# Decode attention over a cached window: all transpositions and scores of a set ahead of the preceding set's V products

## The chip, the cores and the metric

The kernel runs on one core of a Trainium2 chip. The metric is device time in microseconds (us) of one execution, from its first to its last instruction with what lies around them; the median of three runs is 198.4 us (198.16 to 198.71). Engines: TensorE (PE; its weight loads are counted apart as PEld), VectorE (DVE), ScalarE (ACT), GpSimd (POOL) and SyncE (SP), which here only issues DMAs. 16 DMA engines move data between memory and SBUF.

## The reference, cut to what matters

```python
# A: one new token per batch entry, 32 query heads on 8 key/value heads, the last 4096 of 16384 cache rows
q = (x @ wq)                                       # B=4, D=512, Dh=128
k = k_cache[:, :, Sk - 4096:, :];  v = v_cache[:, :, Sk - 4096:, :]
o = softmax(q @ k.T * Dh**-0.5) @ v                # each of 8 kv heads serves 4 query heads
a = o @ wo
# B: a gated two-layer network of the same token
gate = x @ W_gate; up = x @ W_up                   # F = 1792
b = ((gate * (gate > 0)) * up) @ W_down
g = sigmoid((x * gate_w).sum(-1))
out = g * a + (1 - g) * b
```

Nearly all bytes are the two cache windows: 4 x 8 heads x 4096 rows x 128 values in bf16, once for K and once for V, 67 MB of the 81 MB that are read.

## The kernel before, in words

**Tiling.** The 32 pairs of batch entry and kv head are cut into 8 sets of four heads (`NSET`). For each set one DMA loads 4 MB of K into `Ksb[:, s % 2]` and one loads 4 MB of V into `Vsb[:, s % 2]`: 128 partitions of 32 KB each. So there are two K buffers and two V buffers.

**A pass** is one trip through `for s in range(NSET)` (L524). It works on the K of set `s` and on the V of set `s - 1`:

- `kt(s, i)`, i = 0 to 7 (L393): eight PE transpositions (L400) into one of two PSUM tiles `tr`, then one copy back over K in SBUF, by ACT for i in `ACT_TAKES` = 0, 2, 4, 6, 7 (L406), by DVE for 1, 3, 5 (L408). `kt(s, i)` needs the copy of `kt(s, i - 2)`, because of the two tiles.
- `scores(s, bank)`, bank = 0 to 3 (L410): eight matmuls (L422), after the copies of `kt(s, 2*bank)` and `kt(s, 2*bank + 1)`. After banks 1 and 3 DVE adds the mask and takes the maximum (L428); bank 2 needs the first of these two to have read the tile.
- `maximum(s)` (L432): DVE, one PE product (L436), DVE; `exponent(s, k)`, k = 0, 1 (L445): ACT; `turn(s, k)`, k = 0, 1 (L452): DVE transposes the probabilities into `pT`.
- `values(s, k)`, k = 0 to 3 (L457): sixteen matmuls each (L465) of `pT` with V, into the tile `ob`; after the last ACT copies it out (L471).
- `combine(s)` (L474): small PE products (L479, L483) and DVE scaling; `queries(s)` (L383): POOL prepares the query tile.

**The order of the work** is written out by hand. Each engine runs its list in program order; PE, ACT and DVE run the passes as a hardware loop of two passes per turn. L527 to L550 is that order. The pass of set 0 also runs `maximum`, `values` and so on for set -1 and -2, on nothing of use, so that all turns of the loop are alike.

**The loads** all come from SP, in one list: K0; then for s = 1 to 7 K(s) and V(s-1); then W_gate and W_up (into the K buffer 0), V7, W_down, and five pieces of wo, which wait for nothing. SP waits ahead of each load for the buffer to be free, and a wait holds all loads behind it. L267: K(s) waits for `("SC", s - 2, 3)`, the last score matmul of set s - 2. L271: V(s-1) waits for `("PV", s - 3, 3)`, the last V product of set s - 3.

**What SP really waits for.** Each event counts up a semaphore for one kind of receiver. `SC` and `PV` count for DVE and ACT. For another receiver, `need` (L115) takes the next event of that engine in program order that counts for it:

```python
if by is not None and s[1] not in (kind, "all"):
    s = (by, kind)
    n = 1 + sum(1 for k in self.history[s] if k < at)
```

SP is of kind "x". In the passes PE has two events of that kind, ahead of the change: `TOP(s)`, the first transposition of `kt(s, 0)` (L402), and `CMB(s)`, the first product of `combine(s)` (L480). After the score matmuls of bank 3 in pass s - 2 the next is `TOP(s - 1)`, so K(s) waits for the first transposition of the next pass. That transposition itself waits for the arrival of K(s - 1), and is behind `values(s - 3, 3)` and `maximum(s - 2)` on PE. V(s-1) waits for the same `TOP(s - 1)`. W_gate and W_up wait for `TOP(7)`, W_down for `CMB(6)` behind the last pass.

**After the passes** come `maximum`, `exponent` and `turn` of set 7, `combine(6)`, the first layer of B, `values(7, ...)`, `combine(7)`, and the products with W_down and wo (L576, L565), then two copies (L594, L596) and the store.

Of the kernel before, what the change touches and what calls it, by code (L numbers as in the profile page):

```python
# [181 lines left out]
def bass_gated_mix__sliding_block_cached__glu_gated_reglu__decode_kernel(  # L182
# [13 lines left out]
    with ExitStack() as ctx:  # L196
# [196 lines left out]
        def kt(s, i):  # L393
            bk = TR[i % 2]
            for cc in range(8):
                c = 8 * i + cc
                w = []
                if cc == 0:
                    w = [("K", s), ("KTC", s, i - 2) if i >= 2 else ("KTC", s - 1, i - 2 + NFILL)]
                P.op("pe", lambda e, cc=cc, c=c: e.transpose(  # L400
                    bk[:, cc * 128:(cc + 1) * 128], Kw[:, s % 2, c * 128:(c + 1) * 128], identw[:, :]),
                    ("KT", s, i) if cc == 7 else ("TOP", s) if cc == 0 and i == 0 else None, w,  # L402
                    to="x" if cc == 0 else "act" if i in ACT_TAKES else "dve")
            dst = Kw[:, s % 2, i * 1024:(i + 1) * 1024]
            if i in ACT_TAKES:
                P.op("act", lambda e: e.copy(dst, bk[:, :]), ("KTC", s, i), [("KT", s, i)], to="pe")  # L406
            else:
                P.op("dve", lambda e: e.tensor_copy(dst, bk[:, :]), ("KTC", s, i), [("KT", s, i)], to="pe")  # L408

        def scores(s, bank):  # L410
            bk = SCB[bank % 2]
            pair = bank // 2
            k4 = Ksb[:, s % 2, :].rearrange("p (c k o) -> p c k o", k=128, o=2)
            for o in range(2):
                for a in range(4):
                    w = []
                    if a == 0 and o == 0:
                        w = [("KTC", s, 2 * bank + u) for u in range(2)] + [("QS", s)]
                        w.append(("SCC", s, 0) if pair else ("SCC", s - 1, 1))
                        if bank == 0:  # L420
                            w.append(("NEGMAX", s - 1))
                    P.op("pe", lambda e, a=a, o=o: e.matmul(  # L422
                        bk[32 * a:32 * a + 32, 0:512], qS[:, s % 2, 32 * o:32 * o + 32],
                        k4[:, 16 * bank:16 * bank + 16, 32 * a:32 * a + 32, o], start=(o == 0), stop=(o == 1),
                        tile_position=(0, 32 * a)),
                        ("SC", s, bank) if (a == 3 and o == 1 and bank % 2) else None, w, to="dve")
            if bank % 2:
                P.op("dve", lambda e: e.tensor_tensor_reduce(  # L428
                    sc[:, s % 2, pair * 1024:(pair + 1) * 1024], SCP[:, :], mask[:, :], 1.0, LOWEST, ALU.add, ALU.max,
                    mx[:, s % 2, pair:pair + 1]), ("SCC", s, pair), [("SC", s, bank)], to="dve" if pair else "pe")  # L430

        def maximum(s):  # L432
            par = s % 2
            P.op("dve", lambda e: e.tensor_reduce(mcol[:, par:par + 1], mx[:, par, :], AXIS.X, ALU.max),  # L434
                 ("MCOL", s), [("SCC", s, 1)], to="pe")
            P.op("pe", lambda e: e.matmul(SCB[0][:, 0:128], mcol[:, par:par + 1].to_broadcast([128, 128]), identw[:, :],  # L436
                                          start=True, stop=True),
                 ("MT", s), [("MCOL", s)], to="dve")
            P.op("dve", lambda e: e.tensor_tensor_reduce(  # L439
                mrow[:, :], SCB[0][:, 0:128], qmask[:, :], -SCALE, -LOWEST, ALU.add, ALU.min, negmax[:, par:par + 1]),  # L440
                ("NEGMAX", s), [("MT", s)], to="act")
# [3 lines left out]
        def exponent(s, k):  # L445
            par = s % 2
            P.op("act", lambda e: e.activation(  # L447
                sc[:, par, k * PW:(k + 1) * PW], sc[:, par, k * PW:(k + 1) * PW], ACTF.Exp,
                bias=negmax[:, par:par + 1], scale=SCALE, accum_out=rowsum[:, par, k:k + 1]),
                ("EXP", s, k), [("NEGMAX", s)], to="dve")  # L450

        def turn(s, k):  # L452
            par = s % 2
            P.op("dve", lambda e: e.transpose(pT[:, par, k * PW:(k + 1) * PW], sc[:, par, k * PW:(k + 1) * PW]),  # L454
                 ("PTT", s, k), [("EXP", s, k)], to="pe")

        def values(s, k):  # L457
            par = s % 2
            for c in range(16):
                g = c % 4  # L460
                w = []
                if c == 0:
                    w = [("PTT", s, k * NPIECE // 4), ("V", s), ("OSB", s - 1)]
                blk = 16 * k + c
                P.op("pe", lambda e, c=c, g=g, blk=blk: e.matmul(  # L465
                    OB[32 * g:32 * g + 32, 0:256], pT[:, par, 32 * blk:32 * blk + 32],
                    Vsb[:, par, 256 * blk:256 * blk + 256],
                    start=(k == 0 and c < 4), stop=(k == 3 and c >= 12), tile_position=(0, 32 * g)),
                    ("PV", s, k) if c == 15 and k == 3 else None, w, to="act")
            if k == 3:  # L470
                P.op("act", lambda e: e.copy(osb[:, par, :], OB[:, 0:256]), ("OSB", s),  # L471
                     [("PV", s, 3)], to="pe")

        def combine(s):  # L474
            par, b, half = s % 2, s // 2, s % 2
            r = slice(64 * half, 64 * half + 64)
            for k in range(8):
                lo = 3 - k % 4 + 64 * (k // 4)
                P.op("pe", lambda e, k=k, lo=lo: e.matmul(FB[r, 384:416], Wsel[:, lo:lo + 64], osb[:, par, 32 * k:32 * k + 32],  # L479
                                                          start=(k == 0), stop=(k == 7)), ("CMB", s) if k == 0 else None,  # L480
                     [("OSB", s)], to="x")
            for k in range(NPIECE):
                P.op("pe", lambda e, k=k: e.matmul(FB[r, 416:417], Wsum[:, :], rowsum[:, par, k:k + 1],  # L483
                                                   start=(k == 0), stop=(k == NPIECE - 1)),
                     ("SUMS", s) if k == NPIECE - 1 else None, [], to="dve")
            P.op("dve", lambda e: e.reciprocal(recip[r, par:par + 1], FB[r, 416:417]), ("RECIP", s), [("SUMS", s)], to="dve")  # L486
            if s >= NSET - 2:
                P.op("dve", lambda e: e.tensor_scalar(oq[r, 32 * b:32 * b + 32], FB[r, 384:416], recip[r, par:par + 1],
                                                      gsb[r, b:b + 1], op0=ALU.mult, op1=ALU.mult),
                     ("OQ", s), [("RECIP", s)], to="pe")  # L490
                return
            P.op("dve", lambda e: e.tensor_scalar(otmp[r, :], FB[r, 384:416], recip[r, par:par + 1], None, op0=ALU.mult),  # L492
                 ("OQ", s), [("RECIP", s)], to="x")
            if s >= 0 and half == 1:
                P.op("pool", lambda e: e.tensor_scalar(oq[:, 32 * b:32 * b + 32], otmp[:, :], gsb[:, b:b + 1], None, op0=ALU.mult),  # L495
                     ("OQP", s), [("OQ", s)], to="all")
# [27 lines left out]
        for s in range(NSET):  # L524
            if s % 2 == 0:
                P.turn_edge()
            maximum(s - 1)  # L527
            kt(s, 0)
            kt(s, 1)
            exponent(s - 1, 0)  # L530
            kt(s, 2)
            turn(s - 1, 0)
            exponent(s - 1, 1)
            scores(s, 0)
            combine(s - 2)
            if s + 1 < NSET:
                queries(s + 1)
            kt(s, 3)
            turn(s - 1, 1)
            kt(s, 4)  # L540
            scores(s, 1)
            kt(s, 5)
            kt(s, 6)
            scores(s, 2)
            values(s - 1, 0)
            kt(s, 7)
            values(s - 1, 1)
            values(s - 1, 2)
            scores(s, 3)
            values(s - 1, 3)  # L550
        P.turn_edge()
        maximum(NSET - 1)
        for k in range(NPIECE):
# [105 lines left out]
```

## Time and profile before

| what | value |
|---|---|
| median of 3 runs | 198.4 us |
| the profiled execution: its own time | 197.82 us |
| its span, first to last instruction | 196.6 us |
| PE busy, x instructions | 138.3 us (70%), x1752 |
| DVE busy | 79.8 us (41%) |
| ACT busy | 70.1 us (36%) |
| POOL busy | 14.2 us (7%) |
| bytes read | 81.01 MB, 412 GB/s over the span |
| mean granted PE clock | 0.912 |
| chain that ended last: DMA | 61% |
| chain that ended last: PE, DVE, ACT | 19%, 13%, 4% |

The span is cut into 40 slices of 4.9 us on the page, and other views give any stretch. The chain is followed back from the last instruction: each piece names what was waited for. "issue" is time in which nothing was waited for that the profile shows. In rows of the timeline the first number is the start in us from the start of the span, the second the time taken; `x8` counts instructions, and in brackets stands the idle time of the engine ahead of them with what ended it. SPq rows are SP handing a DMA to its queue, not the transfer.

### The profile page before, as it was taken

What the parts mean: (1) busy time and instruction counts of PE and PEld (TensorE: products, weight loads), DVE (VectorE), ACT (ScalarE), POOL (GpSimd) and SP (SyncE); (2) the same over time, 40 slices, a digit from 0 to 9 for tenths busy, and PEclk for the clock granted to TensorE, in tenths of its full rate; (3) what the DMA queues carried; (4) which work ended last, traced back from release to release, by engine and by line L of the source; (5) the groups of instructions that cost most, each with busy time, mean ns of one, the idle gap of its engine ahead of it and who ended that gap; (6) DMA issues with size and microseconds to landing.
All of it is one profiled execution on the core that took longest, in us unless ns stands there. A gap on an engine that the chain in (4) does not pass through costs nothing.

```text
span 196.6 us, 3919 instructions
## 1 busy us (share of the span) xinstructions
PE 138.3 (70%) x1752; PEld 103.7 (53%) x1752; DVE 79.8 (41%) x127; ACT 70.1 (36%) x97; POOL 14.2 (7%) x34
## 2 busy tenths in 40 slices
PE   0145598879769789973988599759986988603964
PEld 0112476567647557751866387629664765403713
DVE  0000058257435925733176346432663582560001
ACT  1105082355228426440452255224522823500011
POOL 6393000000000000100000001000000000000000
PEclk9999999999999999999699969985999999985555
DMA  6999999969999999999999999999999989998991
GB/s 214 440 440 460 453 440 423 433 270 427 440 443 440 427 433 433 427 427 427 427 427 427 427 427 427 440 440 447 440 433 440 433 381 429 477 427 382 422 401 50
DMA packets 3879, 81.10 MB, mean 413 GB/s; under 512 B 409, under 2 KB 930, under 8 KB 1058
## 3 DMA queue, kind: packets, MB, share of 16 engines
q1 hardware_dynamic: 3864, 81.01, 96.5%
q8 instruction: 5, 0.08, 0.2%
q10 hardware_dynamic: 10, 0.01, 0.0%
HBM read 81.01 MB, written 0.00 MB: 412 GB/s over the span
## 4 chain that ended last, share of the span: by engine, by line
DMA 61%; PE 19%; DVE 13%; ACT 4%; issue 1%; SPq 1%; DVEq 0%
DMA Ksb<-in_A_k_cache_dram 49%; DMA Wbig<-in_A_wo_dram 11%; PE tr L400 10%; DVE Ksb L408 5%; DVE zs L428 5%; PE scp L422 4%; ACT Ksb L406 4%; DVE pT L454 2%; PE fb L479 2%; PE scp L565 1%; PE scp L436 1%; PE ob L465 1%; PE fb L483 0%; DVE zs L434 0%; SPq L289 0%
## 5 line engine op out<-in xcount | busy, mean ns | idle before, releaser
L400 PE MATMUL tr<-identw,Ksb 128*128 128x128 f32 x512 | 70.8, 296 | 7.6 <-DMA Ksb<-in_A_k_cache_dram 6.7
L400 PEld LDWEIGHTS tr<-identw,Ksb 128*128 128x128 f32 x512 | 62.2, 152 | 14.9 <-DMA Ksb<-in_A_k_cache_dram 7.9
L406 ACT COPY Ksb<-tr 128x1024 f32<-128x1024 f32 x40 | 40.5, 1012 | 78.2 <-PE tr L400 78.0
L408 DVE COPY Ksb<-tr 128x1024 f32<-128x1024 f32 x24 | 29.4, 1223 | 29.5 <-PE tr L400 29.5
L428 DVE CUSTOM_DVE_ANT_0 zs<-scp,mask 128x1024 bf16<-128x1024 f32 x16 | 19.3, 1205 | 31.2 <-PE scp L422 31.2
L422 PE MATMUL scp<-Ksb,qS 128*32 128x512 bf16 x256 | 20.0, 387 | 13.0 <-DVE Ksb L408 12.1
L465 PE MATMUL ob<-Vsb,pT 128*32 128x256 bf16 x576 | 21.8, 289 | 7.9 <-DMA Vsb<-in_A_v_cache_dram 7.9
L454 DVE STREAM_TRANSPOSE pT<-zs 128x1024 bf16<-128x1024 bf16 x18 | 22.2, 1238 | 1.8 <-ACT zs L447 1.3
L465 PEld LDWEIGHTS ob<-Vsb,pT 128*32 128x32 bf16 x576 | 15.6, 101 | 13.9 <-issue 9.7
L447 ACT ACTIVATE zs<-zs,negmax 128x1024 bf16<-128x1024 bf16 x18 | 20.7, 1150 | 2.0 <-DVE negmax L439 2.0
L422 PEld LDWEIGHTS scp<-Ksb,qS 128*32 128x32 bf16 x256 | 3.9, 95 | 21.2 <-DVE Ksb L408 18.0
L436 PE MATMUL scp<-identw,zs 128*128 128x128 f32 x18 | 4.9, 359 | 12.2 <-DVE zs L434 10.9
L479 PEld LDWEIGHTS fb<-zs 128*64 128x64 f32 x160 | 10.9, 147 | 4.6 <-issue 3.6
L479 PE MATMUL fb<-zs 128*64 128x32 f32 x160 | 12.0, 231 | 0.5 <-ACT zs L471 0.5
L436 PEld LDWEIGHTS scp<-identw,zs 128*128 128x128 f32 x18 | 3.0, 210 | 14.6 <-DVE zs L434 13.1
L471 ACT COPY zs<-ob 128x256 f32<-128x256 f32 x9 | 3.3, 372 | 20.6 <-PE ob L465 20.6
L486 DVE RECIPROCAL recip<-fb 64x1 f32<-64x1 f32 x10 | 1.6, 162 | 17.7 <-PE fb L483 17.7
L384 POOL TENSOR_TENSOR qS<-zs,cmask 128x64 bf16<-128x64 bf16 x8 | 2.4, 306 | 66.8 <-PE tr L400 64.7
L341 PE MATMUL fb<-identw,zs 5*128 5x5 f32 x4 | 0.6, 262 | 8.9 <-POOL zs L308 8.9
L350 DVE RECIPROCAL gsb<-ez 128x4 f32<-128x4 f32 x1 | 0.2, 178 | 16.0 <-POOL ez L349 16.0
L495 POOL TENSOR_SCALAR oq<-otmp,gsb 128x32 bf16<-128x32 f32 x3 | 1.1, 364 | 71.4 <-DVE otmp L492 71.4
L439 DVE CUSTOM_DVE_ANT_0 mrow<-scp,qmask 128x128 f32<-128x128 f32 x9 | 2.6, 292 | 8.1 <-PE scp L436 8.1
(60 smaller groups left out, 55.1 us busy)
## 6 DMA issues: line engine op xcount, KB each, us to landing
Ksb<-in_A_k_cache_dram SPq DMA_DIRECT2D x8, 4096.0 KB, 19.0
Vsb<-in_A_v_cache_dram SPq DMA_DIRECT2D x8, 4096.0 KB, 28.0
Vsb<-in_A_wq_dram SPq DMA_DIRECT2D x1, 4096.0 KB, 12.1
Wbig<-in_A_wo_dram SPq DMA_DIRECT2D x1, 2048.0 KB, 19.2
Ksb<-in_B_W_gate_dram SPq DMA_DIRECT2D x1, 1792.0 KB, 13.6
Ksb<-in_B_W_up_dram SPq DMA_DIRECT2D x1, 1792.0 KB, 17.5
Vsb<-in_B_W_down_dram SPq DMA_DIRECT2D x1, 1792.0 KB, 14.7
Wbig<-in_A_wo_dram SPq DMA_DIRECT2D x1, 1280.0 KB, 21.9
```

The source lines that it names most:

```text
L400: P.op("pe", lambda e, cc=cc, c=c: e.transpose(bk[:, cc * 128:(cc + 1) * 128], Kw[:, s % 2, c * 128:(c + 1) * 128], identw[:, :]), ("KT", ...
L406: P.op("act", lambda e: e.copy(dst, bk[:, :]), ("KTC", s, i), [("KT", s, i)], to="pe")
L408: P.op("dve", lambda e: e.tensor_copy(dst, bk[:, :]), ("KTC", s, i), [("KT", s, i)], to="pe")
L422: P.op("pe", lambda e, a=a, o=o: e.matmul(bk[32 * a:32 * a + 32, 0:512], qS[:, s % 2, 32 * o:32 * o + 32], k4[:, 16 * bank:16 * bank + 16, ...
L428: P.op("dve", lambda e: e.tensor_tensor_reduce(sc[:, s % 2, pair * 1024:(pair + 1) * 1024], SCP[:, :], mask[:, :], 1.0, LOWEST, ALU.add, A ...
L436: P.op("pe", lambda e: e.matmul(SCB[0][:, 0:128], mcol[:, par:par + 1].to_broadcast([128, 128]), identw[:, :], start=True, stop=True), ("M ...
L439: P.op("dve", lambda e: e.tensor_tensor_reduce(mrow[:, :], SCB[0][:, 0:128], qmask[:, :], -SCALE, -LOWEST, ALU.add, ALU.min, negmax[:, par ...
L447: P.op("act", lambda e: e.activation(sc[:, par, k * PW:(k + 1) * PW], sc[:, par, k * PW:(k + 1) * PW], ACTF.Exp, bias=negmax[:, par:par + ...
L454: P.op("dve", lambda e: e.transpose(pT[:, par, k * PW:(k + 1) * PW], sc[:, par, k * PW:(k + 1) * PW]), ("PTT", s, k), [("EXP", s, k)], to= ...
L465: P.op("pe", lambda e, c=c, g=g, blk=blk: e.matmul(OB[32 * g:32 * g + 32, 0:256], pT[:, par, 32 * blk:32 * blk + 32], Vsb[:, par, 256 * bl ...
L471: P.op("act", lambda e: e.copy(osb[:, par, :], OB[:, 0:256]), ("OSB", s), [("PV", s, 3)], to="pe")
L479: P.op("pe", lambda e, k=k, lo=lo: e.matmul(FB[r, 384:416], Wsel[:, lo:lo + 64], osb[:, par, 32 * k:32 * k + 32], start=(k == 0), stop=(k ...
```

## The change

The functions stay as they are. The order inside a pass is written anew: `kt(s, 0)` to `kt(s, 7)` and `scores(s, 0)` to `scores(s, 3)` come first, `exponent`, `turn` and `combine` of the earlier sets stand at other places between them, and `values(s - 1, 0)` to `values(s - 1, 3)` come in one row at the end of the pass. And the first matmul of `values(s, 0)` gets a name of its own, `("VAL", s)`, that counts for receivers of kind "x".

```diff
-                    ("PV", s, k) if c == 15 and k == 3 else None, w, to="act")
+                    ("PV", s, k) if c == 15 and k == 3 else ("VAL", s) if c == 0 and k == 0 else None, w,
+                    to="act" if c == 15 else "x")
...
             maximum(s - 1)
             kt(s, 0)
             kt(s, 1)
+            kt(s, 2)
             exponent(s - 1, 0)
-            kt(s, 2)
+            scores(s, 0)
+            kt(s, 3)
+            kt(s, 4)
+            exponent(s - 1, 1)
+            scores(s, 1)
+            kt(s, 5)
             turn(s - 1, 0)
-            exponent(s - 1, 1)
-            scores(s, 0)
+            turn(s - 1, 1)
+            kt(s, 6)
+            scores(s, 2)
+            kt(s, 7)
             combine(s - 2)
             if s + 1 < NSET:
                 queries(s + 1)
-            kt(s, 3)
-            turn(s - 1, 1)
-            kt(s, 4)
-            scores(s, 1)
-            kt(s, 5)
-            kt(s, 6)
-            scores(s, 2)
-            values(s - 1, 0)
-            kt(s, 7)
-            values(s - 1, 1)
-            values(s - 1, 2)
             scores(s, 3)
-            values(s - 1, 3)
+            for k in range(4):
+                values(s - 1, k)
```

So in pass s - 2 the next event of kind "x" after the score matmuls is now `VAL(s - 3)`, the first V product of the same pass, and K(s) waits for that. It needs V(s - 3) and both `turn(s - 3, ...)`. W_gate and W_up wait for `VAL(5)` in pass 6 in the same way. V(s - 1) still waits for `TOP(s - 1)` and W_down for `CMB(6)`.

## The prediction

> **What bounds the kernel now.** I read the page's slices first (4.9 us each): the busy share of the DMA engines, and what they moved.
>
> ```profile
> DMA  6999999969999999999999999999999989998991
> GB/s 214 440 440 460 453 440 423 433 270 427 440 443 440 427 433 433 427 427 427 427 427 427 427 427 427 440 440 447 440 433 440 433 381 429 477 427 382 422 401 50
> ```
>
> The transfers run at about 430 GB/s from the second slice to the last but one, so the kernel is bound by its 81 MB. The exception is the ninth slice (39.3 to 44.2 us): 270. Then the chain that ended last:
>
> ```profile
> 74.61 19.02 DMA Ksb<-in_A_k_cache_dram
> ...
> 94.17 18.89 DMA Ksb<-in_A_k_cache_dram
> ...
> 113.47 19.03 DMA Ksb<-in_A_k_cache_dram
> ...
> 133.06 18.87 DMA Ksb<-in_A_k_cache_dram
> ...
> 170.37 21.86 DMA Wbig<-in_A_wo_dram
> 192.23 0.04 issue
> 192.27 2.31 PE scp L565 x67
> ```
>
> From 74.6 us on it is a chain of arrivals. K4 to K7 land at 93.63, 113.07, 132.50 and 151.92: one pass per 19.43 us, the time of 8 MB. The end is the arrival of wo and 4.4 us after it. What is worth something is only what makes the stream of transfers end sooner. Where did it stop? Three stretches of 4.9 us (engines' busy time, clock, DMA share, GB/s) and SP in the timeline:
>
> ```profile
> 34.30:39.20 4.90, 4.12 (x88) 2.71 (x88) 1.00 (x2) 1.78 (x3) 0.00 (x0) 1.00 1.02 441
> 39.20:44.10 4.90, 3.65 (x34) 2.97 (x34) 2.75 (x7) 2.79 (x5) 0.31 (x1) 1.00 0.60 231
> 44.10:49.00 4.90, 4.46 (x56) 3.56 (x49) 3.64 (x5) 2.88 (x4) 0.00 (x0) 1.00 1.02 435
> ```
>
> ```profile
> 1.25 1.30 SPq L266 DMA_DIRECT2D Ksb<-in_A_k_cache_dram  x2
> ...
> 2.60 0.60 SPq L270 DMA_DIRECT2D Vsb<-in_A_v_cache_dram  x1
> ...
> 40.55 1.91 PE L400 MATMUL tr<-identw,Ksb 128*128 128x128 f32 x16
> ...
> 40.85 0.53 SPq L266 DMA_DIRECT2D Ksb<-in_A_k_cache_dram  x1
> ```
>
> wq, K0, K1 and V0 are handed over by 3.2 us. K2 is handed over at 40.85, 0.3 us after the first transposition of the second pass (`TOP(1)`). The trace's records of single packets (32 KB, 1.21 us each) show V0's last packets ending at 41.3 to 41.6 us on all engines but one, and K2's first beginning at 42.2 on four engines and at 42.8 to 43.25 on the rest: 1.35 to 2.4 us after the issue. That is the hole. No later load comes so late: K3 is issued at 58.07 and K4 at 74.61, each some 5 us or more before the V transfer ahead of it ends.
>
> **The change, part by part.**
>
> *The release of K2.* Pass 0 begins when K0 lands (22.6 us). I lay out the new order with the durations of this trace: eight transpositions 1.04 us; copies 1.01 (ACT) and 1.23 (DVE); eight score matmuls 0.62; mask and maximum 1.24; exponent 1.15; turn 1.23; combine 1.33. `kt(0)` to `kt(2)` end at 26.8 as now, `scores(0)` at 27.9, `scores(1)` waits for DVE's copy of `kt(3)` and ends at 30.8. DVE then has mask, copy of `kt(5)` and both turns (to 35.6), ACT the copy of `kt(6)` by 33.9. `scores(2)` ends at 33.9, `kt(7)` at 34.9, its copy at 35.9, combine beside it at 36.2, `scores(3)` at 36.85. There `VAL(-1)` begins; its V buffer counts as filled in pass 0. So K2 is issued at about 36.9 instead of 40.85: 4.4 us before V0 ends, where at most 2.4 are needed. The hole closes, with 2 us to spare. V1 stays behind `TOP(1)`, forecast at 39.4 (36.85, 2.2 us of V products, maximum), with K2's 9.7 us ahead of it in the queue.
>
> *What the hole is worth.* By slices: (430 - 270)/430 x 4.9 = 1.8 us. By stretches: (438 - 231)/438 x 4.9 = 2.3 us. By each DMA engine's own completions, the nearest row: the first engine ended V0 at 41.70 and K2 at 52.94, 11.24 us for a transfer that takes 9.71 in all later ones. That is **1.53 us**, and 1.5 to 1.85 for single engines, as they changed places. I take 1.55, and keep 1.2 and 2.3 as ends: a stretch holds only four rounds of packets, so its rate is coarse.
>
> But the last arrival counts, and one engine is late. Five instruction fetches (16 KB, the page's queue q8) run on the same DMA engines, at 32.0, 41.7, 55.6, 184.1 and 194.2 us. Each sets one engine back about 1.5 us: after the first, 15 engines end K1 within 0.3 us and one at 1.8. Today the hole wipes out the first two; the one at 55.6 stays, and every load from V1 on lands 1.5 us after most of its parts. With the hole gone all three stay. In the order of the packets the first, the third and the fourth are on different engines (different places within a round), so they do not add: the latest engine is again 1.8 us after the first.
>
> *Moved within the pass.* In later passes the same sum gives `VAL` 12.9 us and the end of `maximum` 15.6 us after a K lands, where today it is 16.7 (57.77 to 74.44). The period is 19.43. So PE's gain of 1.1 us per pass hides behind the transfers and is worth nothing. No engine gets more work: the instructions are the same. V(s-1) lands 9.7 us into the pass, ahead of `VAL`, so the row of V products does not wait for it.
>
> *Moved past SP's queue.* K(s) from pass 2 on is issued 12.9 us into pass s-2, not at the next landing (19.4). The transfers ahead of it run until 29.1, so from either moment it waits in the queue: nothing. W_gate and W_up likewise. W_down needs `CMB(6)`, today at 169.5; by the sum about 150.4 + 16 = 166.5, while V7 runs to 178: nothing. Behind V7's landing nothing changes.
>
> *Clock.* The idle time of a pass is now gathered at its end: 19.4 - 15.6 = 3.8 us. Two passes today, one with little idle time ahead and full clock, one with the clock at half for 6.8 us around its start (131.3 to 138.1):
>
> ```profile
> 57.70:74.30 16.60, 13.82 (x185) 10.58 (x184) 9.20 (x14) 7.71 (x10) 0.30 (x1) 1.00 0.98 422
> 132.50:151.90 19.40, 16.33 (x182) 12.94 (x182) 9.10 (x14) 7.71 (x10) 0.30 (x1) 0.86 1.00 432
> ```
>
> PE's work took 2.5 us more, 0.37 us for each us at half clock. 6.8 us in every pass would make 15.6 into 18.1, still under 19.43: nothing. The Trainium skill's page TensorE: Matmul & The Clock Gate (HAM oscillation) speaks against the change here: idle gaps over about 3.4 us throttle the array. The trace agrees that the clock falls at waits for K (at three of the four from 93 us on, the shortest of 0.7 us); by that rule every pass starts slow, and the sum is the same.
>
> The other weighed rule is DMA: Bandwidth & Descriptors (Specifications): a first byte about 0.6 us after issue from SP. By it K2's data would have come at 41.45 and the hole be worth 0.2 us; the packets here, at 1.35 to 2.4 us, decide against it.
>
> **Sum.** The profiled execution's 197.82 us (span 196.6) less 1.55 gives 196.27; the median of the runs shown is 0.58 above the profiled one, so 198.4 - 1.55 = **196.85 us**.
>
> **The rivals.**
>
> - *The fetches add up.* If the second fetch's engine, whose place I could not read, is also the third's or the fourth's, that engine is 3 us late instead of 1.5 at the end and the hole's gain is gone: 198.3. For: the hole hid it until now. Against: the three that can be told apart sit on three engines. The Trainium skill's Runtime: NRT & Kernel Launch (Instruction fetch mechanics) has an engine's sequencer fetch 256 instructions at a time on a DMA queue of its own; which DMA engine, it does not say.
> - *K2 still comes late.* Pass 0 is a chain over three engines; if DVE's turns or a copy order push `VAL(-1)` beyond 38.9 us, each us costs one, until 40.85. At 40 us: 198.4 - 0.5 = 197.9. Two places would have to slip by 2 us.
> - *Slower: PE at half clock becomes the bound.* Place: every pass from the fourth on. Price: at half clock throughout, 15.6 + 0.37 x 19.4 = 22.8 us, 3.4 more than the transfers, in five passes 17 us; PE's idle time before V7 lands (172 to 180) takes back 8: 196.85 + 9 = 206. It decides from 10.3 us at half clock per pass ((19.43 - 15.6)/0.37). Against: the most seen is 6.8, and busy passes returned to full clock. For: after 176 us it stayed at 0.50 for 20 us with PE busy 4.4 of 4.9 us.
> - *The hole is worth the stretches' 2.3 us:* 196.1.
>
> **How the numbers follow.** Forecast 0.74; fetches 0.10; late K2 0.07; slower 0.05; larger 0.04. About 0.3% (0.6 us) is what a measurement of this kernel can tell from no change. Faster by more: the forecast, the larger hole, half of late K2 = 0.81. Within: fetches and the other half = 0.13 or 0.14. Slower: 0.05, raised to 0.06 for what I have not seen. The likeliest case's own range is 196.2 to 197.4 (gain 1.2 to 1.85, runs 0.3 apart). The asked range goes from the larger hole, 196.0, to no gain, 198.4.
>
> **What would show it.** Right: K2 issued by SP at 36 to 38.5 us, the ninth slice at 425 or more; K4 to K7 landing some 1.5 us sooner (92.1, 111.5, 131.0, 150.4), still 19.43 apart; PE idle 3 to 4 us ahead of each, with the clock falling at each pass's start and no effect; wo's arrival at 190.7. Wrong: K2 issued past 38.9; landings that are no sooner though the hole is gone (fetches); a period above 19.43 (PE bound); another low slice, above all between 50 and 75 us, where the early K loads now come 5 us sooner and their V loads do not.

## The result, and the profile after

Five runs of the changed kernel take 196.42 us in the median (196.22 to 196.47), five of the kernel before 198.4 (197.9 to 198.71): ratio 0.990, 95% interval 0.989 to 0.992. The change makes the kernel 2 us, or 1%, faster; forecast were 196.85 us and a gain of 1.55. The profiled execution after takes 196.37 us (span 195.0), the one before 197.82.

The slices of the page after, clock of PE ahead of the two lines that answer to those of before:

```profile
PEclk9999589999999996998599979996997599995555
DMA  6999999999999999999999999999999989998992
GB/s 216 437 430 430 437 437 440 437 427 450 433 423 430 437 430 437 430 437 437 430 430 437 430 437 430 437 430 430 430 430 430 430 383 426 481 430 377 431 394 63
```

The ninth slice reads 427 where it read 270. By stretches, at the same places as before (last column GB/s):

```profile
34.30:39.20 4.90, 4.90 (x103) 4.28 (x104) 3.39 (x7) 1.29 (x2) 0.31 (x1) 1.00 1.01 435
39.20:44.10 4.90, 4.67 (x44) 3.78 (x43) 1.59 (x4) 2.81 (x4) 0.00 (x0) 1.00 1.01 431
44.10:49.00 4.90, 3.88 (x41) 2.55 (x38) 4.17 (x5) 3.62 (x6) 0.00 (x0) 1.00 1.01 435
```

The hole is gone. Why, is in the timeline after, end of the first pass:

```profile
36.51 0.62 PE L422 MATMUL scp<-Ksb,qS 128*32 128x512 bf16 x8
...
36.96 1.92 PE L465 MATMUL ob<-Vsb,pT 128*32 128x256 bf16 x64
...
37.26 0.54 SPq L266 DMA_DIRECT2D Ksb<-in_A_k_cache_dram  x1
...
39.13 1.91 PE L400 MATMUL tr<-identw,Ksb 128*128 128x128 f32 x16
...
39.43 0.54 SPq L270 DMA_DIRECT2D Vsb<-in_A_v_cache_dram  x1
```

K2 goes to its queue 0.3 us after the first V product, at 37.26 us; V1, which still waits for the next pass's first transposition, at 39.43. The chain after:

```profile
51.98 20.65 DMA Ksb<-in_A_k_cache_dram
...
86.70 24.78 DMA Ksb<-in_A_k_cache_dram
...
126.02 24.31 DMA Ksb<-in_A_k_cache_dram
...
169.88 20.82 DMA Wbig<-in_A_wo_dram
190.69 0.04 issue
190.74 2.31 PE scp L564 x67
```

The pieces now begin at the early issues and end at the arrivals of K3 (72.63), K5 (111.48) and K7 (150.34): K5 and K7 are each 1.6 us sooner than before, 19.43 us per pass as ever. wo's piece arrives at 190.69, 1.54 sooner, and behind it come the same 2.31 us of PE.

The trace's records of each DMA engine's own completion say more than the arrivals. First engine, last engine, and the distance of the first from that of the load ahead of it; a DMA engine is late when it ends 1.4 us or more behind the first:

```text
            before                       after
         first   last   distance     first   last   distance
V0       41.70  43.54     9.70       41.64  43.64     9.72
K2       52.94  53.50    11.24       51.36  53.19     9.72
V1       62.65  64.49     9.71       61.06  62.91     9.70
K4       91.79  93.63     9.71       90.20  92.05     9.71
V7      178.08 179.94     9.71      176.49 178.34     9.71
late engines at V1:  before 1, after 3
```

### The profile page after: what moved, and what is told of

It reads as the page before. It is cut to its first block, busy times and chain, and to the rows that moved or that the text cites. A ratio compares the mean times of both kernels' runs of the same rounds, so it can differ in the third digit from the quotient of the medians.

```text
span 195.0 us, 3927 instructions
## 1 busy us (share of the span) xinstructions
PE 139.9 (72%) x1752; PEld 108.2 (55%) x1752; DVE 79.7 (41%) x127; ACT 70.1 (36%) x97; POOL 14.2 (7%) x34
## 4 chain that ended last, share of the span: by engine, by line
DMA 57%; PE 25%; DVE 11%; PEld 2%; issue 2%; SPq 1%; ACT 1%; DVEq 0%; PEldq 0%
DMA Ksb<-in_A_k_cache_dram 47%; PE tr L400 14%; DMA Wbig<-in_A_wo_dram 11%; DVE Ksb L408 7%; PE scp L422 6%; DVE zs L428 3%; PE fb L480 2%; PE scp L564 1%; PE ob L465 1%; PEld ob L465 1%; ACT Ksb L406 1%; PEld fb L480 1%; PE scp L436 0%; PEld tr L400 0%; PE fb L484 0%
## 5 line engine op out<-in xcount | busy, mean ns | idle before, releaser
L400 PE MATMUL tr<-identw,Ksb 128*128 128x128 f32 x512 | 74.7, 307 | 14.5 <-DMA Ksb<-in_A_k_cache_dram 14.1
L400 PEld LDWEIGHTS tr<-identw,Ksb 128*128 128x128 f32 x512 | 66.2, 159 | 26.8 <-DMA Ksb<-in_A_k_cache_dram 15.3
L465 PE MATMUL ob<-Vsb,pT 128*32 128x256 bf16 x576 | 18.9, 288 | 6.8 <-DMA Vsb<-in_A_v_cache_dram 6.8
L454 DVE STREAM_TRANSPOSE pT<-zs 128x1024 bf16<-128x1024 bf16 x18 | 21.3, 1220 | 1.3 <-ACT zs L447 1.3
L465 PEld LDWEIGHTS ob<-Vsb,pT 128*32 128x32 bf16 x576 | 16.3, 101 | 9.8 <-issue 7.2
L422 PEld LDWEIGHTS scp<-Ksb,qS 128*32 128x32 bf16 x256 | 3.9, 95 | 15.2 <-DVE Ksb L408 15.1
L358 PE MATMUL scp<-Vsb,zs 128*32 128x512 bf16 x32 | 3.3, 584 | 3.1 <-DMA Vsb<-in_A_wq_dram 3.1
```

Source lines behind the costliest of these rows:

```text
L358: P.op("pe", lambda e, half=half, t=t, g=g, col=col: e.matmul(SCB[half][32 * g:32 * g + 32, 0:512], xT[:, t, 0:32], Wq3[:, t, col:col + 51 ...
L400: P.op("pe", lambda e, cc=cc, c=c: e.transpose(bk[:, cc * 128:(cc + 1) * 128], Kw[:, s % 2, c * 128:(c + 1) * 128], identw[:, :]), ("KT", ...
L422: P.op("pe", lambda e, a=a, o=o: e.matmul(bk[32 * a:32 * a + 32, 0:512], qS[:, s % 2, 32 * o:32 * o + 32], k4[:, 16 * bank:16 * bank + 16, ...
L465: P.op("pe", lambda e, c=c, g=g, blk=blk: e.matmul(OB[32 * g:32 * g + 32, 0:256], pT[:, par, 32 * blk:32 * blk + 32], Vsb[:, par, 256 * bl ...
```

## The experiments

Theory A: the whole gain is the one hole ahead of K2. Theory B: PE's shorter pass, since the V products now cover the mask and maximum of the scores. Theory C: every K load issued earlier, a deeper queue. Kernels e1 to e4 ran on one chip (before: 198.56 us in the median of its runs there), e5 to e8 on a second (198.26), e9 to e12 on the first again (198.32).

**e1: the early release alone.**

```diff
-                    ("PV", s, k) if c == 15 and k == 3 else None, w, to="act")
+                    ("PV", s, k) if c == 15 and k == 3 else ("VAL", s) if c == 0 and k == 3 else None, w,
+                    to="act" if c == 15 else "x")
```

> The old order of the pass is kept; the first matmul of values(s, 3), which stands right behind the last score products, counts for SP, so that K(s) is released there and not by the next pass's first transposition. Theory A (the one hole ahead of K2): K2 is issued at about 38.9 us instead of 40.85, just at the point where the hole closes; 196.4 to 196.9 us against 198.4. Theory B (the shorter pass on PE makes the gain): no change, 198.4. Theory C (every K load issued earlier, a deeper queue): as A, 196.4 to 196.9.

Measured: 197.95 us (196.81 to 198.92), ratio 0.997 (0.994 to 0.999). SP in its timeline:

```profile
39.49 0.54 SPq L266 DMA_DIRECT2D Ksb<-in_A_k_cache_dram  x1
```

A miss for A as I had put it: K2 came at 39.49, not 38.9, as the first pass of this execution ran at half clock until 27.65 us. That is 0.6 us past the point where the hole closes, and some of the hole is there: K2 10.34 us behind V0, and its first packets took 1.7 to 2.0 us on ten engines instead of 1.21. Part of the gain, widely spread; the execution traced took 197.15, and what the longer ones lost is not shown. The run doesn't separate A from C.

**e2: the new order alone** (the change without the name `VAL`).

```diff
-                    ("PV", s, k) if c == 15 and k == 3 else ("VAL", s) if c == 0 and k == 0 else None, w,
-                    to="act" if c == 15 else "x")
+                    ("PV", s, k) if c == 15 and k == 3 else None, w, to="act")
```

> The new order of the pass is kept; the first V product does not count for SP, so K(s) waits for the next pass's first transposition as before. Theory A: K2 is issued when the second pass begins, at about 39.4 us, 0.5 us past the point where the hole closes; the hole shrinks by about two thirds: 196.9 to 197.4 us. Theory B: the whole gain, 196.4. Theory C: no gain, 198.4.

Measured: 197.57 us (197.06 to 198.95), ratio 0.995 (0.993 to 0.998): between the two ends as A had it, though a little above A's 196.9 to 197.4, and K2 0.7 us later than expected. SP:

```profile
40.06 0.54 SPq L266 DMA_DIRECT2D Ksb<-in_A_k_cache_dram  x1
```

The new order by itself shortens the first pass, and with it the hole. Half the gain and not the whole: against B. K loads that still wait for the next pass, and yet a gain: against C alone.

**e3: the hole filled with other bytes, order and releases as before.**

```diff
         for s in range(1, NSET):
+            if s == 2:
+                P.dma("sp", ... Wbig[:, 0:512 * WO_CUTS[1]] ..., ("WO", 0))
             load_k(s)
             load_v(s - 1)
...
-        for k in range(len(WO_CUTS) - 1):
+        for k in range(1, len(WO_CUTS) - 1):
```

> The kernel before, with one move: the first piece of wo (2 MB, waits for nothing) is handed over ahead of K2 instead of behind W_down. Order and releases of the passes stay. The 4.9 us of that piece lie where the hole was, and the same bytes are missing at the end. Theory A: K2 is still issued at 40.85, no hole, the end comes as much sooner as with the change: 196.4 to 196.9 us; K2 lands 4.9 us later than without the piece, at about 56, still ahead of its pass at 57.8. Theories B and C: 198.4.

Measured: 196.13 us (195.85 to 198.82), ratio 0.989 (0.987 to 0.992). Nine of the twelve runs took 195.85 to 196.3, the other three 197.41, 198.55 and 198.82. SP and the slices:

```profile
3.29 0.62 SPq L279 DMA_DIRECT2D Wbig<-in_A_wo_dram  x1
41.51 0.54 SPq L266 DMA_DIRECT2D Ksb<-in_A_k_cache_dram  x1
```

```profile
GB/s 223 438 431 431 445 438 434 411 414 465 438 428 431 445 431 431 431 431 431 431 438 431 431 431 431 431 438 431 431 431 431 431 431 389 433 471 431 390 396 84
```

K2 is issued even later than in the trace of before, the passes are the old ones, and the whole gain is there, because wq, K0, K1, V0 and 2 MB of wo keep the engines busy until 46 us. The last piece of wo lands at 192.56 here, at 192.62 after the change, and at 194.21 before. This is the run that decides against B. The piece also puts 4.9 us more ahead of every later load, so against C stand the distances above, which before the change are 9.7 us everywhere but at K2, and e6 below. Why three of the runs took so much longer is open: e10 and e12 below show a cause for 1.3 us, not for 2.5.

**e4: the kernel before once more**, for a second trace (no edit).

> The kernel before once more, for a second trace of it. The runs of before take 197.9 to 198.7 us, 0.4 us more in the median than what the packets of the one trace explain. If the hole differs from execution to execution, K2's first completion is not 11.24 us behind V0's here but up to 0.8 us away from that, and the arrivals of K4 and later shift by as much. If the 0.4 us lie elsewhere, the distance is 11.2 again and the time differs behind the last arrival or ahead of the first.

Measured: 198.27 us. K2 issued at 41.39, 11.52 us between V0 and K2, K4's first engine 0.31 later than in the other trace, the time 0.45 more. So the hole differs from execution to execution. Set against the other profiled executions whose last loads are the same (hole = distance of K2 from V0 less 9.71; e7, without a hole, took 196.25; e3, e10 and e12 end with other loads, and e11 has a cost of its own):

```text
              K2 issued   hole    time    time less hole
before          40.85     1.53   197.82      196.29
e4 (before)     41.39     1.81   198.27      196.46
e8              41.26     1.74   198.18      196.44
e9              41.12     1.67   197.92      196.25
e6              43.24     3.94   199.99      196.05
e1              39.49     0.63   197.15      196.52
e2              40.06     0.75   197.82      197.07
after           37.26     0      196.37      196.37
e5 (after)      37.58     0      196.38      196.38
```

Less the hole all but one lie within 0.5 us, for holes of 0 to 3.94 us: a us of hole costs about a us of time. In e2 one engine was held by a single packet of 2.5 us behind the hole and stayed 2.7 us late.

**e5: the changed kernel again** (no edit).

> The changed kernel once more, beside the next three on one chip. With the hole closed the executions should lie close together, at about 196.4 us, where those of before spread from 197.8 to 199.8; theory A': the spread of before comes from the hole, because the PE clock's phase in the first pass moves K2's issue (40.85 us in one trace, 41.39 in the other, where the clock came back to full 1.0 us later).

Measured: 196.3 us (196.23 to 196.38), ratio 0.991 (0.989 to 0.992); before on this chip spreads from 197.67 to 198.79. With the hole the spread goes, as expected.

**e6: the release 2 us later**, on the kernel before.

```diff
-                    ("KT", s, i) if cc == 7 else ("TOP", s) if cc == 0 and i == 0 else None, w,
-                    to="x" if cc == 0 else "act" if i in ACT_TAKES else "dve")
+                    ("KT", s, i) if cc == 7 else ("TOP", s) if cc == 6 and i == 1 else None, w,
+                    to="x" if cc == 6 else "act" if i in ACT_TAKES else "dve")
```

> The kernel before, with the event that releases the loads moved from the first transposition of a pass to the last but one of its second eight: K2 is issued some 1.9 us later, at 42.8 to 43.3, and every later load by as much after its pass begins. Theory A: the hole grows by 1.9 us and the time with it, to 200.3; the later loads still wait in the queue, so nothing is added for them. Theory C (every K load's issue counts): 1.9 us for each of several loads, 202 and more. Theory B: 198.4.

Measured: 199.83 us (199.23 to 200.25), ratio 1.008 (1.006 to 1.010): 1.6 us more, of 1.9 expected. SP and slices:

```profile
43.24 0.54 SPq L266 DMA_DIRECT2D Ksb<-in_A_k_cache_dram  x1
...
62.02 0.54 SPq L266 DMA_DIRECT2D Ksb<-in_A_k_cache_dram  x1
```

```profile
GB/s 218 449 462 435 435 429 419 422 168 369 422 419 422 422 475 462 435 422 422 422 422 422 422 422 481 455 429 429 422 422 422 422 414 436 417 442 421 439 389 63
```

Again one low place, at K2, now wider; K3 at 62.02 and all later ones cost nothing (their distances stay at 9.7), though each was issued 3 us and more later than in either trace of before. That speaks against C.

**e7: a longer pass**, on the changed kernel, behind its V products.

```diff
             for k in range(4):
                 values(s - 1, k)
+            for n in range(16):
+                P.op("pe", lambda e: e.transpose(OB[:, 256:384], identw[:, :], identw[:, :]), None,
+                     [("OSB", s - 1)] if n == 0 else [])
```

> The changed kernel with sixteen idle transpositions of the identity matrix behind the V products of each pass, which wait for the copy of their sums: 2.2 us of work and 0.4 of waiting on PE per pass, nothing of it before K2's issue. A pass then takes PE about 18.2 us, still under the 19.43 of its transfers. Theory A: no change, 196.4 (0.3 either way). Theory B: two thirds and more of the gain is gone, 197.8 or later, and up to 2.6 us per pass.

Measured: 196.34 us (196.25 to 196.49), beside 196.30 without it. In its timeline (L551 is the added work):

```profile
90.35 1.92 PE L465 MATMUL ob<-Vsb,pT 128*32 128x256 bf16 x64
92.74 1.97 PE L551 MATMUL ob<-identw 128*128 128x128 f32 x16 [0.48 <-ACT zs L472]
96.14 0.49 PE L436 MATMUL scp<-identw,zs 128*128 128x128 f32 x2 [1.43 <-issue]
96.46 1.91 PE L400 MATMUL tr<-identw,Ksb 128*128 128x128 f32 x16
```

K4 had landed at 92.0 there; PE begins its pass 4.5 us late and nothing is lost, since K6 is released from within the pass and the queue still holds V3 and K5. Its passes take PE 17.1 and 18.8 us in turn, more than the 16.7 and 17.4 of the kernel before, and the gain is still whole: against B. What PE gains per pass is worth nothing, and it can lose these 2.4 us per pass at no cost. (It also ran at full clock until 175 us, at equal time.)

**e8 and e9: PE kept busy ahead of the first pass**, on the kernel before, with 20 and 40 transpositions.

```diff
+        for n in range(20):     # e9: 40
+            P.op("pe", lambda e, n=n: e.transpose(TR[1][:, 128 * (n % 8):128 * (n % 8) + 128], identw[:, :], identw[:, :]),
+                 None, [("IDENTW",)])
         def queries(s):
```

> The kernel before with twenty idle transpositions of the identity matrix on PE ahead of the passes, from about 18.2 to 21 or 22 us, while K0 is still on its way, so that PE is busy where it was idle and the first pass begins nearer to full clock. Theory A': K2 is issued at 39.8 to 40.4 us in every execution, the hole is smaller by about 0.5 to 1 us, the time 197.4 to 197.9 and the spread of the executions narrower. If the clock of the first pass has no part in it: 198.4 with the spread of before.

> As the run with twenty idle transpositions, which left PE idle for 2.4 us before K0 came and the first pass at half clock until 26.1 us, but with forty, so that PE is busy until about 22.6 us. Theory A' (the phase of the clock in the first pass moves K2's issue): full clock from the first transposition, K2 issued at 39.9 to 40.4 us, the hole 0.6 to 1 us smaller, 197.2 to 197.8 us against 198.3, and a narrower spread. Else: 198.3 and the spread of before. If the clock falls all the same, K2 comes no earlier and the run tells nothing.

Measured: 197.91 us (196.93 to 199.53), ratio 0.999 (0.996 to 1.001); and 198.22 (197.9 to 198.71), ratio 1.000 (0.999 to 1.001). Neither is a test of what it was made for. In e8 the clock was at half from 22.7 to 26.1 all the same. In e9 it was at full, but the first sixteen of the added transpositions had run at half clock (213 ns from one to the next, then 109), and the work took too long:

```profile
18.06 6.20 PE L384 MATMUL tr<-identw 128*128 128x128 f32 x40
24.09 0.39 PE L440 MATMUL scp<-identw,zs 128*128 128x128 f32 x2
24.31 1.91 PE L404 MATMUL tr<-identw,Ksb 128*128 128x128 f32 x16
```

The pass began at 24.3 instead of 22.6 us, and K2 was issued at 41.12. For the clock's part in the spread of before there remain the traces side by side: with the old order, half clock ended at 25.45, 26.11, 26.40, 26.73 and 26.92 us (before, e8, e4, e12, e3), and K2 was issued at 40.85, 41.26, 41.39, 41.46 and 41.51. That fits; no run shows it alone. That e8's runs spread wider than those of before is not explained.

**e10 and e12: the piece of wo ahead of K2, with the new order and with the old** (the edit of e3, on the changed kernel and on the kernel before).

> The changed kernel, and the first piece of wo handed over ahead of K2. There is no hole left to fill, so theory A expects nothing for the transfers: 196.3, or up to 0.4 sooner as in the run with the old order and the piece, whose PE clock was full in the last stretch because V7 lands 4.9 us later and PE has less time to idle ahead of it: 195.9 to 196.3.

> The kernel before with the first piece of wo ahead of K2, once more, beside the changed kernel with the same piece on one chip. Theory A: 196.1, within 0.3 of the changed kernel, so the order of the passes adds nothing to it. If the order of the passes has a part of its own, it stays behind the run with both by more than 0.3.

Measured: 196.15 us (195.92 to 197.47), ratio 0.989 (0.987 to 0.991), and 196.18 (196.06 to 197.66), ratio 0.990 (0.988 to 0.993). Order and release add nothing to the filled hole: A again. In the median both are 0.1 to 0.3 us ahead of the change, but single runs are 1.2 us behind it. The two profiled executions show why; first e10 (197.47 us), then e12 (196.2), from V7's landing:

```profile
183.47 3.60 PE L467 MATMUL ob<-Vsb,pT 128*32 128x256 bf16 x64 [4.93 <-DMA Vsb<-in_A_v_cache_dram]
...
187.54 1.92 PE L482 MATMUL fb<-zs 128*64 128x32 f32 x16 [0.48 <-ACT zs L474]
...
192.86 0.59 ACT L580 COPY bulk<-scp 128x512 f32<-128x512 f32 x1 [5.37 <-PE scp L577]
```

```profile
183.58 3.60 PE L467 MATMUL ob<-Vsb,pT 128*32 128x256 bf16 x64 [6.78 <-DMA Vsb<-in_A_v_cache_dram]
...
187.66 1.12 PE L481 MATMUL fb<-zs 128*64 128x32 f32 x16 [0.47 <-ACT zs L473]
...
190.86 0.59 ACT L581 COPY bulk<-scp 128x512 f32<-128x512 f32 x1 [3.25 <-PE scp L578]
```

With the piece gone from the end, V7 lands 5 us later and PE's work behind it ends just with the last arrival (192.7 us), or some 1.3 us later when the clock stays at half (until 192.1 in e10, until 187.2 in e12). So this version is no clear gain over the change; a smaller piece, which would fill the hole and leave more at the end, was not tried.

**e11: PE's loop written out**, on the changed kernel.

```diff
-        with eng.Fori(0, len(t) - 1):
+        def turn():
             self.emit_list(eng, sems, engine, ops[t[0]:t[1]], shift(0), {})
...
+        if engine == "pe":
+            for _ in range(len(t) - 1):
+                turn()
+        else:
+            with eng.Fori(0, len(t) - 1):
+                turn()
```

> The changed kernel with PE's four turns of the loop written out instead of looped; the other engines loop as before. PE's program is about three times as long, so about 11 instruction fetches of 16 KB run beside the loads instead of 5. If each fetch sets another DMA engine back by 1.5 us, some ten engines are late together and the end stays: 196.3 to 196.6. If fetches come back to the same engine, one is late by 3 us or more and the end with it: 197.8 or later.

Measured: 197.91 us (197.77 to 198.89), 1.5 us more than the changed kernel's 196.42. Its queues on the page:

```profile
q1 hardware_dynamic: 3864, 81.01, 96.5%
q8 instruction: 14, 0.23, 0.5%
```

14 fetches instead of 5. The first eight each make another engine late by about 1.5 us, and the end stays where it was; the next ones come back to engines that are late already: each of the ninth to the thirteenth adds one to the engines that are 3 us late. At the last load eight engines are late, three by 1.7 to 1.9 us and five by 3.0 to 3.3. So the fetches do add up, but only from the ninth on. K2 was issued at 37.33 and there was no hole: this is a cost of its own.

## Why the prediction was right, point by point

- **What bounds the kernel, and the hole as the only place that counts:** right. e3 gives the whole gain with nothing but the hole closed, e6 makes it wider and loses as much, e7 takes back PE's gain and loses nothing. Open remain the wide spreads of e1, e3 and e8.
- **The release of K2:** forecast 36.9, measured 37.26 in one trace and 37.58 in the other. The durations added up: the first V product came at 36.96 and 37.28, where the sum had 36.85. Left out were the 0.3 us from that product to the issue, which the traces show here as at `TOP(1)` before; the rest fits the longer half clock at the pass's beginning, until 26.1 and 27.8 us instead of 25.45. (In `values`, `VAL` waits for `turn(s, 0)` alone and not, as said ahead of the prediction, for both; both had ended at 35.9.) The point where the hole closes, 38.9, held: at 39.49 (e1) part of it was back.
- **What the hole is worth:** the mechanism was right and the size too small. 1.55 us was the hole of one execution, and between the two profiled executions the forecast of 196.27 met 196.37. In the median the change brings 1.98 us, on the second chip 1.96. The step that failed is "the median of the runs shown is 0.58 above the profiled one, so 198.4 - 1.55": the distance of 0.58 was carried over to the kernel after as if the change left it, but the kernel after has no such distance (its profiled run 196.37, its median 196.42). Part of it is itself hole: e4 had 1.81 and took 0.45 us more, 0.28 of it hole. The rest is not traced. So the gain of 1.98 lies above the 1.2 to 1.85 of the likeliest case, though the time lies within its 196.2 to 197.4; the lower end of the asked range came from the stretches' 2.3 us.
- **Late engines:** right. Three engines are late after, one before, all by 1.5 us and more, and the last arrival is that of one late engine either way. (The fetches stand 0.3 us earlier in the trace than the prediction has them, at 31.7, 41.4, 55.3, 183.8 and 193.9; nothing hangs on it.) The rival (fetches add up) is real but far off: it takes nine fetches (e11), and this kernel has five.
- **Moved within the pass, worth nothing:** right (e7, e10 against e12). The gain itself was rough: at full clock a pass took PE 14.9 instead of 16.7 us as the first of a loop's turn and 16.45 instead of 17.4 as the second, where the loop's edge adds 1.3 to 1.5 us that the sum lacked. PE's time spent waiting for K went from 6.7 to 14.1 us over the passes.
- **Moved past SP's queue, worth nothing:** right. K3 to K7 were issued 6 to 7.5 us sooner and landed 1.5 to 1.6 us sooner, which is what K2's first engine had gained (1.58); K2 itself landed only 0.3 us sooner, because two late engines end it. V1 to V6 stayed behind their `TOP`, no other slice fell.
- **Clock:** right in effect. In the profiled executions the clock fell at five passes instead of three between 30 and 175 us, and its mean over the execution went from 0.912 to 0.873. But that is not the change's doing alone: the other four runs after had 0.903 to 0.931, and e5's trace fell at three passes. Nor does the length of a wait decide it: the clock fell at waits for K of 0.7 to 2.0 us before and 1.4 to 3.3 us after, all under the 3.4 us that the prediction quotes, and e5 waited 2.1 and 3.2 us without a fall. K6 was released 15.1 us after K4's landing rather than 12.9, in a pass at half clock, and W_down issued at 169.03 rather than 166.5: half clock and a loop edge. All of it beside transfers. The slower rival would have needed 10.3 us at half clock per pass; the most seen was 6.8.
- **The page's first byte:** K2's first packets came 1.35 us after the issue in e2 too, and 1.33 in e6. The Trainium skill's DMA: Bandwidth & Descriptors (Specifications) has about 0.6 us, by which e2, issued at 40.06 with V0's packets ending from 41.2 us on, would have had no hole; it had one of 0.75 us.

## What to carry to other kernels

In a kernel that its transfers bound, look for the one place where the queue runs dry, and price it by each DMA engine's own completions: here 1.5 to 2 us of 198, from a single wait, while passes made shorter by 0.9 to 1.8 us brought nothing. Compare each load's issue with the end of the last transfer ahead of it. K5 to K7 waited for the landing of the load ahead and cost nothing, because a V load was still under way; K2, at the end of the first pass, came when the last transfer was all but done. Such a load has to be released by an earlier event, one of the pass that frees its buffer; or bytes that wait for nothing go in front of it. And one profiled execution can have a small hole: when the runs spread by more than a us, take the size from several traces.

## What the runs showed of the hardware that I had not expected

- Behind a queue that ran dry the first packets are slow: K2's took 1.7 to 2.1 us on four to ten engines (before, e4, e1) where 32 KB otherwise take 1.21. The last arrival can lose more or less than the first engine's hole: K4 landed 0.8 to 0.9 us later than without a hole in e1 (0.63), and 1.6 us later in e4 (1.81).
- An instruction fetch of 16 KB takes 0.9 to 1.2 us of one DMA engine, and the packet beside it 0.5 us more; the engine stays late by 1.5 us until the end of a stream that has no holes. Eight fetches in a row met eight different engines (e11). With 20 transpositions more ahead of the passes (e8) the first fetch came at 26.9 instead of 31.7 to 31.9 us, and with PE's loop written out there were 14 fetches: it is PE's own program that is fetched.
- A hole lets late engines catch up: before, K2's completions lie within 0.6 us though two engines were late at V0, after within 1.8.
